# A gated linear attention, spectral mixer and conv gate on one core: the state update computed for each head's own 48 value columns only

## The chip, the cores and the metric

The kernel runs on one core of one Trainium2 chip. A core has a matrix engine (TensorE, in the profile PE, with its weight loads listed apart as PEld), a vector engine (VectorE, DVE), an activation engine (ScalarE, ACT), a general engine (GpSimd, POOL) and a synchronisation engine (SP) that issues the transfers here. They run side by side, each through its own list of instructions in order, and wait for each other by semaphores. SBUF is the working memory of 128 partitions; PSUM is the small memory that the matrix engine writes to. The metric is the device time of one execution in microseconds (us).

## The reference

Three stages follow one another on float32 data: a gated linear attention over 4 batches, 8 heads, 768 time steps and head dimension 48; a spectral mixer over time and channels; and a feed-forward part with a convolution of three taps and a gate. The change is in the first one.

```python
def _attn_ref(q, k, v, alpha):
    B, H, S, D = q.shape                       # 4, 8, 768, 48
    state = np.zeros((B, H, D, D))
    for t in range(S):
        state = alpha[:, :, t, :, None] * state + np.einsum('bhd,bhe->bhde', k[:, :, t], v[:, :, t])
        y[:, :, t] = np.einsum('bhd,bhde->bhe', q[:, :, t], state)

def _moe_ref(x, w_theta, w_tok_r, w_tok_i, w_ch):
    theta = x @ w_theta
    y = einsum('ts,bsd->btd', w_tok_r, x * cos(theta)) + einsum('ts,bsd->btd', w_tok_i, x * sin(theta))
    u = x + y
    return u + maximum(u @ w_ch, 0)

def _moe2_ref(x, w_in, conv_w, w_out):
    h = maximum(x @ w_in, 0)
    return (h * sigmoid(conv3(h, conv_w))) @ w_out
```

Each head has a state of 48 by 48 numbers. A head's state never meets another head's values.

## The kernel before

The 768 time steps of a batch are cut into 6 chunks of 128 (`NC`), so there are 24 chunks, numbered `ci`. Below, chunk n is the chunk with `ci` = n; chunks 0 to 5 are batch 0, 6 to 11 batch 1. Heads go in pairs: a tile holds the 48 channels of one head in partitions 0 to 47 and those of its partner in partitions 64 to 111 (a "column tile of 64" for the matrix engine), for 4 pairs (`NP`).

For each chunk, `a_prep` runs two scans on the vector engine (L229, L234), each of 4 segments of 129 columns, and multiplies q and k by their results (L243). `a_score` transposes k (`kps`, L252), makes the scores (`sc`), copies them (`pt`, L261) and masks them on GpSimd (L262). `a_y` makes the output of the chunk in PSUM: 32 matrix instructions from the masked scores (`y<-v_t,pt`, 48 columns) and, from the second chunk of a batch on, 16 from the state (`y<-S,qk_t`, 96 columns). `a_xt` transposes it (`xps`) and copies it to `u` (L321). `a_theta` makes the sines and cosines: `zh` (a rounded copy by ScalarE and the remainder by the vector engine, L71 to L73), the product `th`, then L343 to L348, then again a rounded copy `zh` and a remainder `zl`. `m_mix` is the mixing over time (`yps`); `u<-yps` (L374) empties its PSUM tiles.

The state update stands in the second half of `a_y`. A product of k (transposed, `kt`) and the values goes to the PSUM tile `kv`, in 8 matrix calls, each of which becomes 2 instructions, so 16 for a chunk. The values of both heads of the pair, 96 columns, are multiplied with either head's k, so half of what arises is never used. `tst` = old state + `kv` over partitions 0 to 111 and all 384 columns is one vector instruction (L296). Then GpSimd multiplies, once for each half of the partitions, the head's own 48 columns of each pair by the decay of the next chunk (`ftot`) into the new state `S` (L304). In the first chunk of a batch there is no old state: ScalarE copies the two used halves of `kv` into `S` (L301), and GpSimd multiplies in place.

The order on each engine is not the order of the source. The program is laid out by a scheduler that simulates times of its own, so a change in a few instructions moves others. All small PSUM tiles (`kps`, `sc`, `y`, `kv`, `xps`, `th`) share five buffers of one pool (`ps_a`) in turn: a new one waits until the reader of the fifth last one is done. The mixing has three buffers of its own (`ps_m`). The scan L229 writes a tile with one buffer (`fbt`), which the ScalarE instruction L240 reads, so the scan of a chunk waits for the L240 of the chunk before it.

From about 262 us on, the attention is over, and the rest (mixing of the last batch, `cps`, `hps`, `ops`) is the feed-forward part.

Of the kernel before, what the change touches and what calls it, by code (L numbers as in the profile page):

```python
# [8 lines left out]
F32 = mybir.dt.float32  # L9
# [6 lines left out]
ALU = mybir.AluOpType  # L16
PSUM = bass.MemoryType.PSUM

P = 128
B, H, S, D = 4, 8, 768, 48  # L20
DM = H * D
DFF = 1024
NP = H // 2
# [21 lines left out]
def tile_gated_linear_attention__then__spectral_moe__then__conv_gate(  # L45
# [14 lines left out]
    nc = tc.nc  # L60
    NCH = B * NC

    def mm(o, lhsT, rhs, start, stop):
        nc.tensor.matmul(o, lhsT, rhs, start=start, stop=stop, skip_group_check=True)  # L64
# [34 lines left out]
    def body(top, slow):  # L99
# [46 lines left out]
        with ExitStack() as ph1:  # L146
# [27 lines left out]
            def apool(name, bufs, **kw):  # L174
                return att_ctx.enter_context(tc.tile_pool(name=name, bufs=bufs, **kw))
# [4 lines left out]
            att = None if slow else apool("att", 2, side="right")  # L180
            x_p = apool("x", XB, side="right")
            zf_p = apool("zf", ZF, side="right")
            ps_a = apool("ps_a", 5, space=PSUM)
# [85 lines left out]
            def a_y(ci):  # L269
                qh, kh, ftot, vt = prep.pop(ci)  # L270
                pts, kt = scored.pop(ci)
                c = ci % NC
                Sp, Sn = Sst[ci % 2], Sst[(ci + 1) % 2]
                y = ps_a.tile([P, DM], F32, tag="a", name="y")
                halves = [slice(64 * i, 64 * i + 64) for i in range(2)]
                for p in range(NP):
                    for j in range(2):
                        h = 2 * p + j
                        for t in halves:
                            mm(y[t, h * D : (h + 1) * D], pts[j][:, p, t], vt[:, h * D : (h + 1) * D], h == 0, c == 0)  # L280
                if c > 0:
                    for p in range(NP):
                        for t in halves:
                            mm(y[t, p * 96 : p * 96 + 96], qh[:, p, t], Sp[:, p, :], False, True)
                x = x_p.tile([P, DM], F32, tag="x", name="x")
                marks["x"] = nc.scalar.copy(x, y)
                xs[ci] = x
                if c < NC - 1:
                    kv = ps_a.tile([P, NP, 2 * D], F32, tag="a", name="kv")
                    for p in range(NP):  # L290
                        for t in halves:
                            mm(kv[t, p, :], kt[:, p, t], vt[:, p * 96 : p * 96 + 96], p == 0, True)
                    nft = prep[ci + 1][2]
                    if c > 0:
                        tt = att.tile([P, NP, 2 * D], F32, tag="tst", name="tst", bufs=1)
                        nc.vector.tensor_tensor(tt[:112], Sp[:112], kv[:112], ALU.add)  # L296
                    else:
                        tt = Sn
                        for j in range(2):
                            r = slice(64 * j, 64 * j + D)  # L300
                            nc.scalar.copy(Sn[r, :, j * D : (j + 1) * D], kv[r, :, j * D : (j + 1) * D])  # L301
                    for j in range(2):
                        r = slice(64 * j, 64 * j + D)
                        nc.gpsimd.tensor_tensor(  # L304
                            Sn[r, :, j * D : (j + 1) * D],
                            tt[r, :, j * D : (j + 1) * D],
                            nft[r].unsqueeze(2).to_broadcast([D, NP, D]),
                            ALU.mult,
                        )
# [66 lines left out]
            def a_att(b, c):  # L376
                ci = b * NC + c
                if slow:
                    xs[ci] = x_p.tile([P, DM], F32, tag="x", name="x")
                    nc.sync.dma_start(out=xs[ci], in_=x_dram[b, c * P : (c + 1) * P, :])  # L380
                    a_xt(ci)
                    return
                if ci + 2 < NCH:
                    a_load(ci + 2)
                if ci + 1 < NCH:
                    a_prep(ci + 1)
                    a_score(ci + 1)
                a_y(ci)
                a_xt(ci)
# [306 lines left out]
```

## Time and profile before

| | us |
|---|---|
| median of 3 runs | 580.08 (578.15 to 581.35) |
| the profiled execution | 579.94 |
| its span, first to last instruction | 578.2 |
| PE busy | 553.1 (96%) |
| PEld busy | 532.9 (92%) |
| DVE busy | 457.1 (79%) |
| ACT busy | 338.4 (59%) |
| POOL busy | 93.6 (16%) |

The mean granted clock of TensorE is 0.978 of full speed. A line of a timeline gives the start, the length, the engine, the source line, the operation, what it writes and reads, its size and how many in a row were merged (x16); in square brackets stands how long the engine was idle before it and what ended that. The length of merged matrix instructions reaches to the modelled end of the last one, which overlaps the next instruction's start; so the pace is read from start to start. Times of GpSimd are rough.

### The profile page before, as it was taken

How to read it: one execution, taken by the hardware profiler on the slowest of the kernel's cores; microseconds unless marked ns; L12 is line 12 of the kernel's file. 1: busy time of each engine (PE TensorE's matmuls, PEld its weight loads, DVE VectorE, ACT ScalarE, POOL GpSimd, SP SyncE). 2: the span in 40 equal slices, each digit the busy share in tenths (PEclk: the TensorE clock that was granted, in tenths of full speed). 3: DMA queues.
4: the chain of work that ended last, by engine and by line, in shares of the span. 5: the costliest groups of instructions: out<-in, count | busy, mean ns of one | idle time of the engine just before them, and what ended most of it. 6: DMA issues, size and time to landing. Idle time of an engine off the chain costs nothing.

```text
span 578.2 us, 10973 instructions
## 1 busy us (share of the span) xinstructions
PE 553.1 (96%) x4407; PEld 532.9 (92%) x4407; DVE 457.1 (79%) x688; ACT 338.4 (59%) x695; POOL 93.6 (16%) x99
## 2 busy tenths in 40 slices
PE   6878989989999999999999999999999999999995
PEld 3767879979999999999999999999999999999995
DVE  7899997899856676542658889997888889798780
ACT  3665655555864567542752345567776776667561
POOL 2447514341044400350000000000000000000000
PEclk9688998999999999999999999999999999999999
DMA  8454652564024500320014333401044544546001
GB/s 322 153 170 136 212 187 81 174 220 161 1 83 139 174 20 8 97 64 1 1 31 160 111 112 109 145 20 41 5 147 139 176 137 144 198 143 204 27 29 46
DMA packets 24986, 65.41 MB, mean 113 GB/s; under 512 B 2528, under 2 KB 8672, under 8 KB 24544
## 3 DMA queue, kind: packets, MB, share of 16 engines
q1 hardware_dynamic: 24928, 64.64, 33.9%
q8 instruction: 36, 0.59, 0.4%
q14 instruction: 22, 0.18, 0.1%
HBM read 59.92 MB, written 4.72 MB: 112 GB/s over the span
## 4 chain that ended last, share of the span: by engine, by line
PE 80%; DVE 3%; issue 1%; ACT 1%; ACTq 0%
PE yps L64 23%; PE hps L64 18%; PE ops L64 18%; PE cps L64 7%; PE th L64 5%; PE y L64 4%; PE sc L64 3%; PE kv L64 2%; PE xps L320 1%; PE kps L252 1%; DVE fbt L229 1%; DVE stage L116 1%; DVE fbt L234 0%; DVE wtok L73 0%; DVE stage L115 0%
## 5 line engine op out<-in xcount | busy, mean ns | idle before, releaser
L64 PE MATMUL yps<-wtok,zh 128*128 128x384 f32 x576 | 153.0, 343 | 0.0
L64 PEld LDWEIGHTS yps<-wtok,zh 128*128 128x128 f32 x576 | 105.2, 191 | 2.4 <-ACT pt L261 0.2
L64 PE MATMUL hps<-x,win 128*128 128x386 f32 x576 | 107.1, 339 | 0.0
L64 PE MATMUL ops<-wout,g 128*128 128x384 f32 x576 | 106.9, 338 | 0.0
L64 PEld LDWEIGHTS hps<-x,win 128*128 128x128 f32 x576 | 102.2, 189 | 0.0
L64 PEld LDWEIGHTS ops<-wout,g 128*128 128x128 f32 x576 | 101.7, 187 | 0.0
L64 PE MATMUL yps<-wtok,zl 128*128 128x384 f32 x288 | 96.9, 339 | 0.0
L262 POOL TENSOR_SCALAR_AFFINE_SELECT pt<-pt 128x512 f32<-128x512 f32 x48 | 53.8, 1142 | 147.6 <-ACT pt L261 147.6
L64 PEld LDWEIGHTS yps<-wtok,zl 128*128 128x128 f32 x288 | 54.4, 189 | 0.8
L521 ACT ACTIVATE cv<-cv 128x384 f32<-128x384 f32 x64 | 33.4, 523 | 32.1 <-DVE cv L518 32.1
L229 DVE TENSOR_TENSOR_SCAN fbt<-a_t,onehot 128x516 f32<-128x516 f32 x24 | 29.5, 1229 | 22.9 <-ACT a_t L240 21.2
L73 DVE TENSOR_TENSOR g<-cv,g 128x384 fp32r<-128x384 f32 x64 | 35.5, 555 | 14.8 <-ACT g L72 14.2
L64 PE MATMUL th<-wth,zh 128*128 128x384 f32 x216 | 44.0, 340 | 0.0
L515 DVE SCALAR_TENSOR_TENSOR cv<-hh,cw,cv 128x383 f32<-128x383 f32 (+1 forms) x64 | 38.3, 613 | 4.4 <-ACT cv L512 4.1
L522 DVE SCALAR_TENSOR_TENSOR cv<-cv,hh 128x384 f32<-128x384 f32 x64 | 35.2, 556 | 7.9 <-ACT cv L521 5.9
L512 ACT ACTIVATE cv<-hh,cw 128x384 f32<-128x384 f32 x64 | 38.3, 616 | 3.8 <-DVE g L73 3.3
L64 PE MATMUL cps<-us,wch 128*128 128x384 f32 x216 | 40.3, 339 | 0.0
L72 ACT CAST g<-cv 128x384 fp32r<-128x384 f32 x64 | 32.6, 509 | 11.6 <-DVE cv L522 10.1
L518 DVE SCALAR_TENSOR_TENSOR cv<-hh,cw,cv 128x384 f32<-128x384 f32 (+1 forms) x64 | 38.4, 614 | 0.7
L64 PEld LDWEIGHTS cps<-us,wch 128*128 128x128 f32 x216 | 38.0, 188 | 0.5 <-issue 0.3
L64 PEld LDWEIGHTS th<-wth,zh 128*128 128x128 f32 x216 | 37.4, 188 | 0.5 <-DVE zh L73 0.4
L64 PE MATMUL sc<-qk_t 48*128 48x128 f32 x384 | 34.3, 294 | 3.1 <-DVE tst L296 2.5
(84 smaller groups left out, 826.8 us busy)
## 6 DMA issues: line engine op xcount, KB each, us to landing
qk_t<-in_qka_dram SPq DMA_DIRECT2D x24, 512.0 KB, 4.6
stage<-in_w_tok_dram SPq DMA_DIRECT2D x12, 768.0 KB, 4.5
top<-in_w_tok_dram SPq DMA_DIRECT2D x12, 768.0 KB, 4.3
a_t<-in_qka_dram SPq DMA_DIRECT2D x24, 260.0 KB, 2.8
v_t<-in_v_dram SPq DMA_DIRECT2D x24, 192.0 KB, 3.9
out_dram<-ob SPq DMA_DIRECT2D x24, 192.0 KB, 1.9
stage<-in_w_in_dram SPq DMA_DIRECT2D x4, 768.0 KB, 5.8
stage<-in_w_out_dram SPq DMA_DIRECT2D x4, 768.0 KB, 4.4
```

The source lines that it names most:

```text
L64: nc.tensor.matmul(o, lhsT, rhs, start=start, stop=stop, skip_group_check=True)
L72: cast = nc.scalar.copy(hi, src)
L73: lo_eng.tensor_tensor(lo, src, hi.bitcast(F32), ALU.subtract)
L116: nc.vector.scalar_tensor_tensor(fb, hi, 0xC0000000, fb, ALU.bitwise_and, ALU.bitwise_or)
L229: nc.vector.tensor_tensor_scan(bf[:, AW:0:-1], at[:, AW:0:-1], of[:, AW:0:-1], 0.0, ALU.mult, ALU.add)
L252: nc.tensor.transpose(kps[:, p, :], kh[:, p, :], ident)
L262: nc.gpsimd.affine_select(pt, pt, [[0, NP], [1, P]], ALU.is_ge, 0.0, base=0, channel_multiplier=-1)
L512: nc.scalar.activation(cv, hh[:, o : o + HALF], AF.Copy, scale=cw[:, f, 1:2])
L515: nc.vector.scalar_tensor_tensor(cv[:, a:HALF], hh[:, o + a - 1 : o + HALF - 1], cw[:, f, 0:1], cv[:, a:HALF], ALU.mult, ALU.add)
L518: nc.vector.scalar_tensor_tensor(cv[:, 0:e], hh[:, o + 1 : o + 1 + e], cw[:, f, 2:3], cv[:, 0:e], ALU.mult, ALU.add)
L521: nc.scalar.activation(cv, cv, AF.Tanh, scale=0.5)
L522: nc.vector.scalar_tensor_tensor(cv, cv, 1.0, hh[:, o : o + HALF], ALU.add, ALU.mult)
```

## The change

The tile `kv` is 48 columns wide for each pair instead of 96. Each of the 8 matrix calls takes only the values of the head whose k it uses, so 16 instructions of 48 columns stand where 16 of 96 stood. `tst` is compact too: 48 columns for each pair. It is made by two vector instructions, one for each half of the partitions (48 partitions, 192 columns each), where one of 112 partitions and 384 columns stood. GpSimd's two instructions read the compact tile. In the first chunk of a batch one ScalarE copy of 112 partitions and 192 columns fills `tst`, where two copies of 48 partitions and 192 columns into `S` stood, and GpSimd then writes `S` from `tst`.

```diff
-                    kv = ps_a.tile([P, NP, 2 * D], F32, tag="a", name="kv")
+                    kv = ps_a.tile([P, NP, D], F32, tag="a", name="kv")
                     for p in range(NP):
-                        for t in halves:
-                            mm(kv[t, p, :], kt[:, p, t], vt[:, p * 96 : p * 96 + 96], p == 0, True)
+                        for j, t in enumerate(halves):
+                            h = 2 * p + j
+                            mm(kv[t, p, :], kt[:, p, t], vt[:, h * D : (h + 1) * D], p == 0, True)
                     nft = prep[ci + 1][2]
-                    if c > 0:
-                        tt = att.tile([P, NP, 2 * D], F32, tag="tst", name="tst", bufs=1)
-                        nc.vector.tensor_tensor(tt[:112], Sp[:112], kv[:112], ALU.add)
-                    else:
-                        tt = Sn
-                        for j in range(2):
-                            r = slice(64 * j, 64 * j + D)
-                            nc.scalar.copy(Sn[r, :, j * D : (j + 1) * D], kv[r, :, j * D : (j + 1) * D])
+                    tt = att.tile([P, NP, D], F32, tag="tst", name="tst", bufs=1)
+                    if c == 0:
+                        nc.scalar.copy(tt[:112], kv[:112])
                     for j in range(2):
                         r = slice(64 * j, 64 * j + D)
+                        if c > 0:
+                            nc.vector.tensor_tensor(tt[r], Sp[r, :, j * D : (j + 1) * D], kv[r], ALU.add)
                         nc.gpsimd.tensor_tensor(
                             Sn[r, :, j * D : (j + 1) * D],
-                            tt[r, :, j * D : (j + 1) * D],
+                            tt[r],
                             nft[r].unsqueeze(2).to_broadcast([D, NP, D]),
                             ALU.mult,
                         )
```

The scheduler lays out the changed program anew. Three places matter here; source lines behind the change stand two lower than before. The first is the matrix engine around the state update of chunk 2, where `wtok_84` and `wtok_85` are the two parts of the mixing weights. Before:

```order
L64 MATMUL y<-S_111,qk_t 64x96 x8
L64 MATMUL kv<-v_t,kt 64x96 x8
L320 MATMUL xps<-ident,x 128x128 x3
L64 MATMUL th<-wth_115,zh 128x384
L64 MATMUL th<-wth_116,zh 128x384
```

and now:

```order
L64 MATMUL y<-S_111,qk_t 64x96 x8
L64 MATMUL kv<-v_t,kt 64x48 x8
L64 MATMUL yps<-wtok_84,zh 128x384
L64 MATMUL yps<-wtok_85,zh 128x384
L64 MATMUL yps<-wtok_84,zh 128x384
L64 MATMUL yps<-wtok_85,zh 128x384
L64 MATMUL yps<-wtok_84,zh 128x384
L64 MATMUL yps<-wtok_85,zh 128x384
L318 MATMUL xps<-ident,x 128x128 x3
```

Six mixing instructions of chunk 0 now stand ahead of the transpose of chunk 2. The second place is ScalarE in the same stretch, from the last step of the cosines of chunk 0 on (`zh<-zf` is the rounded copy that those six read). Before:

```order
L347 ACTIVATE zf<-zf,halfpi 128x384
L261 COPY pt<-sc 128x512 x2
L286 COPY x<-y 128x384
L266 COPY kt<-kps 128x512
L72 CAST zh<-zf 128x768
L321 COPY u<-xps 128x3x128
L72 CAST wtok_84<-stage 128x2x384
L240 ACTIVATE a_t,bacc<-fbt 128x1030
```

and now:

```order
L345 ACTIVATE zf<-zf,halfpi 128x384
L261 COPY pt<-sc 128x512
L72 CAST zh<-zf 128x768
L261 COPY pt<-sc 128x512
L286 COPY x<-y 128x384
L266 COPY kt<-kps 128x512
L319 COPY u<-xps 128x3x128
L72 CAST wtok_84<-stage 128x2x384
L240 ACTIVATE a_t,bacc<-fbt 128x1030
```

The rounded copy has moved ahead of the second score copy; `u<-xps` and L240 follow it as before. The third place is the vector engine at the end of batch 1's attention (144 to 151 us before). Before:

```order
L243 TENSOR_TENSOR qk_t<-qk_t,fbt 128x1024
L73 TENSOR_TENSOR zh<-u,zh 128x384
L348 TENSOR_TENSOR zf<-x,zf 128x768 x2
L73 TENSOR_TENSOR zh<-u,zh 128x384
L374 TENSOR_TENSOR u<-yps,u 128x384
L73 TENSOR_TENSOR zl<-zf,zh 128x768
L374 TENSOR_TENSOR u<-yps,u 128x384
```

and now:

```order
L243 TENSOR_TENSOR qk_t<-qk_t,fbt 128x1024
L346 TENSOR_TENSOR zf<-x,zf 128x768 x2
L73 TENSOR_TENSOR zl<-zf,zh 128x768
L73 TENSOR_TENSOR zh<-u,zh 128x384
L372 TENSOR_TENSOR u<-yps,u 128x384
L73 TENSOR_TENSOR zl<-zf,zh 128x768
```

The first remainder `zh` (chunk 9) has gone from here to a place some 6 us earlier, and the second one (chunk 10) now stands behind a `zl`. In the same stretch the matrix engine's list has the products `th` of chunks 6 to 9 in one run of 36, then 36 `yps`, then the `th` of chunk 10.

## Rows read from the trace of the kernel before

**Rows 1.** Stages: us, PE, PEld, DVE, ACT, POOL busy (x instructions), PEclk, DMA, GB/s.

```profile
27.40:97.20 69.80, 59.95 (x606) 54.64 (x607) 68.87 (x82) 43.46 (x88) 32.23 (x21) 0.90 0.51 162
97.20:133.30 36.10, 34.22 (x447) 31.42 (x443) 31.39 (x38) 19.27 (x42) 14.56 (x17) 1.00 0.59 186
133.30:262.00 128.70, 128.70 (x1373) 123.15 (x1373) 88.87 (x111) 78.39 (x161) 36.95 (x44) 1.00 0.25 81
262.00:578.20 316.20, 310.14 (x1803) 308.79 (x1801) 245.19 (x431) 183.10 (x377) 0.12 (x1) 1.00 0.29 97
```

**Rows 2.** Waits of the matrix engine: us in total, times, longest.

```profile
PE y L64 <- POOL S L304: 3.7, 2, 2.6
```

**Rows 3.** Timeline of the vector engine, chunks 2 and 3.

```profile
41.12 0.54 DVE L296 TENSOR_TENSOR tst<-S,kv 112x384 f32<-112x384 f32 x1
41.58 0.94 DVE L116 SCALAR_TENSOR_TENSOR stage<-stage 128x768 uint32<-128x768 uint32 x1
...
45.05 1.22 DVE L229 TENSOR_TENSOR_SCAN fbt<-a_t,onehot 128x516 f32<-128x516 f32 x1
46.20 0.79 DVE L73 TENSOR_TENSOR zh<-u,zh 128x384 fp32r<-128x384 f32 x1
...
47.38 0.17 DVE L233 RECIPROCAL starts<-fbt 128x4 f32<-128x4 f32 x1
47.58 1.23 DVE L234 TENSOR_TENSOR_SCAN fbt<-a_t,starts 128x516 f32<-128x516 f32 x1
...
53.25 0.56 DVE L296 TENSOR_TENSOR tst<-S,kv 112x384 f32<-112x384 f32 x1 [0.29 <-PE kv L64]
```

**Rows 4.** Groups by line and shape: busy us, mean ns, idle before.

```profile
L117 DVE SCALAR_TENSOR_TENSOR stage<-stage 128x768 uint32<-128x768 uint32 x22 | 21.2, 962 | 0.3
...
L296 DVE TENSOR_TENSOR tst<-S,kv 112x384 f32<-112x384 f32 x16 | 8.7, 544 | 6.2 <-PE kv L64 6.2
...
L117 DVE SCALAR_TENSOR_TENSOR stage<-stage 128x384 uint32<-128x384 uint32 x2 | 1.1, 558 | 0.0
```

**Rows 5.** Timeline of GpSimd: the state's two instructions in chunks 2 and 13.

```profile
41.74 5.62 POOL L304 TENSOR_TENSOR S<-tst,ftot 48x192 f32<-48x192 f32 x2 [0.95 <-DVE tst L296]
...
170.04 1.08 POOL L304 TENSOR_TENSOR S<-tst,ftot 48x192 f32<-48x192 f32 x2
```

**Rows 6.** Timeline around chunk 2: matrix engine and ScalarE.

```profile
39.59 0.55 PE L320 MATMUL xps<-ident,x 128*128 128x128 f32 x3 [1.09 <-ACT x L286]
...
40.32 0.84 ACT L72 CAST zh<-zf 128x768 fp32r<-128x768 f32 x1 [0.29 <-DVE zf L348]
41.06 0.47 ACT L321 COPY u<-xps 128x384 f32<-128x384 f32 x1
...
42.16 1.07 ACT L240 ACTIVATE a_t<-fbt 128x1030 bf16<-128x1030 f32 x1
```

**Rows 7.** Timeline of the matrix engine, chunks 6 and 7.

```profile
86.21 1.55 PE L64 MATMUL kv<-v_t,kt 128*64 128x96 f32 x16 [2.63 <-DVE zf L344]
87.69 2.29 PE L64 MATMUL yps<-wtok,zh 128*128 128x384 f32 x6
89.77 0.84 PE L320 MATMUL xps<-ident,x 128*128 128x128 f32 x3
...
95.85 1.14 PE L64 MATMUL y<-v_t,pt 128*64 128x48 f32 x32
96.82 0.85 PE L64 MATMUL y<-S,qk_t 128*64 128x96 f32 x16
97.50 0.83 PE L64 MATMUL kv<-v_t,kt 128*64 128x96 f32 x16
```

**Rows 8.** Timeline at 144 to 148 us: vector engine and matrix engine.

```profile
144.64 1.87 DVE L348 TENSOR_TENSOR zf<-x,zf 128x768 f32<-128x768 f32 x2
146.43 0.55 DVE L73 TENSOR_TENSOR zh<-u,zh 128x384 fp32r<-128x384 f32 x1
...
147.37 0.94 DVE L73 TENSOR_TENSOR zl<-zf,zh 128x768 fp32r<-128x768 f32 x1
...
147.04 1.48 PE L64 MATMUL th<-wth,zh 128*128 128x384 f32 x7
```

## The prediction

> **What bounds the kernel now.** I read the table by stages first. Its third and fourth rows show a matrix engine that is busy throughout from 133 to 262 us, and all but 6 us of the rest [rows 1]: there the time is the sum of its instructions, and the vector engine, at 89 of 129 us, has room. Its first row shows the opposite for 27 to 97 us: the vector engine is busy 68.87 of 69.80 us, while the matrix engine lacks 9.9 us and is granted 0.90 of its full clock. Between, from 97 to 133 us, the vector engine has 31.4 of 36.1 us, and the matrix engine lacks 1.9. The matrix engine's last large gap, 2.63 us before chunk 6's `kv`, is ended by a vector instruction [rows 7]. So a delay of the vector engine before 86 us reaches the end undiminished, unless matrix work shrinks; one at 105 to 130 us reaches it nearly; one after 151 us costs nothing; and a shorter matrix instruction pays only where that engine is the late one, from 86 to 103 us and from 133 us on.
>
> **The matrix instructions.** In chunk 7, start to start, 32 instructions of 48 columns take 0.97 us (30 ns each) and 16 of 96 columns 0.68 us (42.5 ns) [rows 7]. Sixteen at 30 ns take 0.48, so a chunk saves 0.20 us. The ten state updates after 133 us save 2.0 us. [...] The bounds are no saving at all (if loading the weights sets the pace) and half the time, 0.34 us for a chunk.
>
> **Two vector instructions for one.** The trace has no vector instruction of 192 columns. From 768 to 384 columns one kind falls from 962 to 558 ns, 1.05 ns a column [rows 4]; 192 fewer than 544 ns gives 0.34 us. Neighbours without a wait overlap by 0.08 us: L296 starts at 41.12 and the next at 41.58, 0.46 later [rows 3]. If the two halves overlap like that, they take 2 x 0.26 = 0.53, 0.07 more than now. If each starts only when the one before is done, at a distance of 0.03 as L234 behind L233 (47.55 to 47.58), they take 2 x 0.37 = 0.74, 0.28 more. I take 0.28: the halves start in different partitions, and every vector row of before starts at partition 0, so the overlap seen there need not hold.
>
> [...]
>
> **GpSimd between them.** In chunk 2 GpSimd's two state instructions take 5.62 us, against 1.08 in chunk 13 [rows 5]. [...] Chunks 1 to 4 give 4 x 0.43 = 1.7 us. [...]
>
> [...]
>
> In chunks 8 to 10 (105 to 130 us) GpSimd already delays the vector engine after `tst`, so only the 0.28 is new: 3 x 0.28 = 0.85 us. After 151 us nothing counts.
>
> **Chunk 2's new order.** The six `yps` need the rounded copy `zh`, which ends at 41.16 now [rows 6] and about 0.3 later then (chunk 1's delay). The matrix engine, done with `kv` at about 38.2, stands for over 3 us, where now it goes on with `xps` at 39.59. After 2.63 us of standing it ran at half pace: six `yps` in 2.08 us [rows 7]. So 41.5 + 2.1, then `xps` with 0.64: `u<-xps` starts at 44.3 instead of 41.06. L240 starts 1.10 behind it [rows 6] or a little more, at 45.5, and ends at 46.6; the scan L229 waits for it. The vector engine would be there at 45.05 + 0.33 + 0.43 = 45.8. It stands for 0.8 to 0.9 us. If the matrix engine were back at full pace at once, this would be near 0; I take 0.9. By the time of chunk 3's `kv` (about 51.2 by the same steps) the matrix engine has caught up, so the vector engine's wait of 0.29 at 53.25 [rows 3] goes: -0.3.
>
> **Chunk 10's remainder.** At 147.04 the matrix engine's `th` starts 0.06 us after `zh` ends at 146.98 [rows 8]: no slack. In the new order (one `zh` gone, one `zl` put in front) this `zh` ends at about 147.8, before other delays. The matrix engine has by then two instructions fewer behind it, 0.17 us each. 0.8 + 0.35 = 1.15 us are lost for good; the bound on the other side is 0.
>
> **Chunk 0.** One ScalarE copy less (0.33 us) is mostly lost, since the next instruction there waits for the vector engine: -0.1. The later three first chunks have ScalarE to spare.
>
> The sum: 1.7 + 0.9 - 0.3 - 0.1 = +2.2 at 86 us; -0.6 to 103 us; +0.85 to 130 us; +1.15 at 147 us; -2.0 to the end: **+1.6 us**. The profiled execution took 579.94 (span 578.2 and 1.7 around it), so 581.5; it lies 0.14 below the median, so **581.7**, 0.3% slower. The measurement can tell about 0.5% (2.9 us) from no change: under 577.2 is faster, over 583.0 slower.
>
> **Rivals.**
> 1. *The matrix saving decides (faster).* The halves overlap (4 x 0.07), GpSimd doesn't get between, chunk 2's gap is covered and chunk 10's `zh` is too: 0.3 - 0.3 - 0.1 - 0.6 + 0.2 - 2.0 = -2.5, so 577.6. For it speaks that the matrix engine bounds 445 us of the span; against it, that four covers must all hold. Chance 0.19.
> 2. *Chunk 2's gap leaves the matrix engine slow until `kv` of chunk 3 (slower).* If it stays at half pace, then from 44.2: nine `th` 3.1, `kps` 0.85, four `yps` 1.4, 16 `sc` 2.9, 32 `y` 1.75, 16 `y<-S` 1.3 and `kv` 0.9 end at 56.4. The vector engine needs `kv` at 53.3, and waits 3.1 us: 584.8. It decides from where the engine reaches `kv` after 53.3. For it: chunk 6's half pace lasted from 86.2 past `xps` at 89.77 [rows 7]. Against it: the chunk's later instructions are dense. Chance 0.16.
> 3. *The change doesn't shorten `kv`:* the 64-column weight loads set the pace, 42 ns stay, the 2.6 us of savings go: 584.3. Against it, the 30 ns of `y` with the same weight loads. Chance 0.05.
>
> **How the numbers follow.** My forecast has 0.60, with its own range 579.2 to 584.2 (the bounds of the four delays, mostly one or two of them off). Rival 1 reaches below 577.2 in over half of its cases and the forecast hardly does: faster 0.14. Slower takes rivals 2 and 3 (0.19) and a quarter of the forecast's 0.60: 0.34. The rest, 0.52, is no change. The range of 8 in 10 reaches from near the centre of rival 1 to just beyond rival 2: 577.4 to 585.4.
>
> **What would show it.** Right: `kv` of 16 in about 0.5 us start to start from 160 us on; `tst` twice, at a distance of about 0.37, and the following vector instruction longer by about 0.2 in chunks 1 to 4; the first GpSimd half short (0.5 us) there and the second long; a matrix gap of about 3 us before the first `yps` and an idle vector engine before chunk 3's L229; the `th` of chunk 10 waiting for DVE `zh`; the last gap before chunk 6's `kv` ending near 88.4. Wrong: that gap ending at 86 or earlier, a `kv` that stays at 0.68 us, or new gaps of the matrix engine after 160 us, which I hold to be nil.

## The result and the profile after

The changed kernel takes 582.97 us (median of 9 runs, 582.30 to 584.55), the kernel before 579.63 beside it (9 runs, 578.13 to 581.62). The ratio is 1.0054, 95% interval 1.0037 to 1.0072: 3.1 us slower (2.1 to 4.2). The forecast was 581.7 with 1.6 us of loss, its range 577.4 to 585.4. The profiled execution took 582.52, span 580.7. In the runs further down, one execution of 883.58 us and one of the kernel before of 680.48 us, at granted clocks of 0.556 and 0.745, are left out of medians and ratios.

The stages of the kernel after, with the columns of [rows 1]:

```profile
27.40:97.20 69.80, 57.31 (x592) 52.77 (x593) 68.94 (x85) 42.02 (x84) 19.52 (x21) 0.88 0.51 164
97.20:133.30 36.10, 32.70 (x445) 29.40 (x442) 32.18 (x42) 17.99 (x38) 12.61 (x16) 1.00 0.55 178
133.30:262.00 128.70, 126.95 (x1370) 121.41 (x1370) 91.08 (x118) 79.30 (x162) 35.21 (x41) 1.00 0.27 84
262.00:580.70 318.70, 311.74 (x1821) 310.44 (x1817) 246.53 (x434) 183.37 (x379) 2.20 (x5) 1.00 0.29 96
```

The first stage is still the vector engine's (68.94 of 69.80 us). GpSimd fell from 32.23 to 19.52. New is the third row: where the matrix engine had no gap, it now lacks 1.75 us of its 128.70.

Matrix engine, chunks 6 and 7, answering [rows 7]; idle time and what ended it in brackets. First the row behind chunk 7's `kv` in the kernel before, then the kernel after:

```profile
98.25 0.45 PE L64 MATMUL yps<-wtok,zh 128*128 128x384 f32 x1
```

```profile
87.69 1.05 PE L64 MATMUL kv<-v_t,kt 128*64 128x48 f32 x16 [2.02 <-DVE zf L342]
...
97.78 0.62 PE L64 MATMUL kv<-v_t,kt 128*64 128x48 f32 x16
98.33 0.44 PE L64 MATMUL yps<-wtok,zl 128*128 128x384 f32 x1
```

The 16 instructions take 0.55 us start to start (97.78 to 98.33), where they took 0.75 (97.50 to 98.25): the 0.20 of the forecast. Chunk 6's `kv` starts 1.48 later than before.

Vector engine, chunks 1 to 3, answering [rows 3]:

```profile
33.02 0.73 DVE L301 TENSOR_TENSOR tst<-S,kv 48x192 f32<-48x192 f32 x2
33.78 0.98 DVE L73 TENSOR_TENSOR wtok<-stage,wtok 128x768 fp32r<-128x768 f32 x1
34.68 1.53 DVE L229 TENSOR_TENSOR_SCAN fbt<-a_t,onehot 128x516 f32<-128x516 f32 x1
36.14 0.53 DVE L73 TENSOR_TENSOR zh<-u,zh 128x384 fp32r<-128x384 f32 x1
...
44.05 1.11 DVE L117 SCALAR_TENSOR_TENSOR stage<-stage 128x768 uint32<-128x768 uint32 x1
45.08 1.26 DVE L73 TENSOR_TENSOR wtok<-stage,wtok 128x768 fp32r<-128x768 f32 x1
46.27 1.22 DVE L229 TENSOR_TENSOR_SCAN fbt<-a_t,onehot 128x516 f32<-128x516 f32 x1
```

The pair takes 0.73 us and the next instruction starts 0.76 after the pair's start, where one instruction gave 0.46: 0.30 more. The state's GpSimd instructions, answering [rows 5]:

```profile
33.44 1.68 POOL L302 TENSOR_TENSOR S<-tst,ftot 48x192 f32<-48x192 f32 x2 [5.20 <-DVE tst L301]
...
43.84 1.68 POOL L302 TENSOR_TENSOR S<-tst,ftot 48x192 f32<-48x192 f32 x2
```

Both halves are through in 1.68 us, where chunk 2 took 5.62. In chunk 1 the first starts 0.42 after the pair's start, and the vector instruction beside it is hardly longer (0.98, where the kernel before has 0.95); the second holds the scan up by 0.30 (1.53 against 1.23), and `zh` no longer pays (0.53 where [rows 3] has 0.79). In chunk 2 the first starts at 43.84, 0.55 after the pair's start, and the instruction beside it takes 1.11 us, where such an instruction takes some 0.95 without a neighbour [rows 3]; the one beside the second takes 1.26. The matrix engine's wait for S [rows 2] is gone from the waits.

Around chunk 2, answering [rows 6], with ScalarE's rows below the matrix engine's:

```profile
41.96 1.31 PE L64 MATMUL yps<-wtok,zh 128*128 128x384 f32 x6 [2.02 <-ACT zh L72]
43.11 0.55 PE L318 MATMUL xps<-ident,x 128*128 128x128 f32 x3
...
43.70 0.48 ACT L319 COPY u<-xps 128x384 f32<-128x384 f32 x1 [0.44 <-PE xps L318]
...
44.81 1.06 ACT L240 ACTIVATE a_t<-fbt 128x1030 bf16<-128x1030 f32 x1
```

L240 ends at 45.87, the scan follows at 46.27, and the vector engine does not stand. Answering [rows 8], at 148 to 151 us:

```profile
149.73 0.61 PE L64 MATMUL th<-wth,zh 128*128 128x384 f32 x2 [1.29 <-ACT zh L72]
150.78 1.50 PE L64 MATMUL th<-wth,zh 128*128 128x384 f32 x7 [0.43 <-DVE zh L73]
...
149.17 0.51 ACT L72 CAST zh<-u 128x384 fp32r<-128x384 f32 x1
...
150.18 0.55 DVE L73 TENSOR_TENSOR zh<-u,zh 128x384 fp32r<-128x384 f32 x1
```

Here the matrix engine stands for 1.29 us, until ScalarE's copy `zh<-u` of 149.17 is done, and for 0.43 us, until the vector engine's remainder is. And a gap that no term of the forecast has, in the feed-forward part:

```profile
360.38 4.92 PE L64 MATMUL cps<-us,wch 128*128 128x384 f32 x27
366.33 2.00 PE L64 MATMUL cps<-us,wch 128*128 128x384 f32 x10 [1.03 <-ACT us L72]
```

### The profile page after: what moved, and what is told of

Read it like the earlier page. It is cut to its first block, busy times and chain, and to the rows that moved or that the text cites. A ratio compares the mean times of both kernels' runs of the same rounds, so it can differ in the third digit from the quotient of the medians.

```text
span 580.7 us, 11015 instructions
## 1 busy us (share of the span) xinstructions
PE 548.2 (94%) x4407; PEld 529.0 (91%) x4407; DVE 460.7 (79%) x704; ACT 337.0 (58%) x691; POOL 79.1 (14%) x99
## 4 chain that ended last, share of the span: by engine, by line
PE 75%; DVE 6%; issue 2%; DMA 1%; ACT 1%
PE yps L64 21%; PE hps L64 18%; PE ops L64 18%; PE cps L64 7%; PE th L64 4%; PE y L64 4%; PE sc L64 2%; PE kv L64 1%; DMA stage<-in_w_tok_dram 1%; DVE fbt L234 1%; PE xps L318 1%; DVE stage L116 1%; DVE fbt L229 1%; PE kps L252 1%; DVE wtok L73 1%
## 5 line engine op out<-in xcount | busy, mean ns | idle before, releaser
L64 PE MATMUL yps<-wtok,zh 128*128 128x384 f32 x576 | 150.8, 341 | 3.2 <-ACT zh L72 2.0
L262 POOL TENSOR_SCALAR_AFFINE_SELECT pt<-pt 128x512 f32<-128x512 f32 x48 | 52.5, 1114 | 169.4 <-ACT pt L261 169.3
L64 PE MATMUL th<-wth,zh 128*128 128x384 f32 x216 | 47.0, 356 | 1.7 <-ACT zh L72 1.3
L64 PEld LDWEIGHTS th<-wth,zh 128*128 128x128 f32 x216 | 39.7, 199 | 2.8 <-ACT zh L72 1.6
```

The source lines that it names most:

```text
L262: nc.gpsimd.affine_select(pt, pt, [[0, NP], [1, P]], ALU.is_ge, 0.0, base=0, channel_multiplier=-1)
```

## The experiments

The program builder puts the instructions into another order as soon as `kv` is 48 columns wide, whether the sum is one vector instruction or two. So the change has three parts: the width of `kv`, the pair, and the order. The runs take them one by one. The runs with `in_order` in their diffs hold every engine to a listed order by dependences without a wait; their line numbers stand 107 to 109 higher, those of the others a few at most. The pair alone and the narrow product with one sum in the new order have no list: the builder gives them these orders by itself, the new one exactly on the matrix and vector engines, the old one but for a single instruction each on the matrix engine, ScalarE and the vector engine. "Both, in the old order" has this same order. In all of them but the change itself and the run on chunk 2, the first chunk of a batch keeps the two ScalarE copies of the kernel before.

| run | `kv` columns | sums | order | ratio to before, 95% | us |
|---|---|---|---|---|---|
| pair alone | 96 | 2 | old | 1.0024, 1.0005 to 1.0043 | +1.4 |
| narrow alone | 48 | 1 | old | 0.9959, 0.9931 to 0.9987 | -2.4 |
| narrow alone, again | 48 | 1 | old | 0.9949, 0.9920 to 0.9978 | -3.0 |
| both | 48 | 2 | old | 1.0001, 0.9979 to 1.0023 | +0.1 |
| the change, again | 48 | 2 | new | 1.0072, 1.0033 to 1.0110 | +4.2 |
| narrow, one sum | 48 | 1 | new | 1.0027, 1.0001 to 1.0053 | +1.6 |
| new order alone | 96 | 1 | new | 1.0064, 1.0038 to 1.0089 | +3.7 |

The last column is the ratio less 1, times 580. Each ratio is to the kernel before on the same chip; the runs stand on three chips, so ratios are compared, not times. The kernel before held to its own list was not run; that a list by itself costs nothing is shown only so far that the stretch from chunk 12's `kv` to the first `cps` takes 159.0 us in the changed kernel and also in the one run of it with a list.

### The pair alone

```diff
-                        nc.vector.tensor_tensor(tt[:112], Sp[:112], kv[:112], ALU.add)
+                        for j in range(2):
+                            r = slice(64 * j, 64 * j + D)
+                            js = slice(j * D, (j + 1) * D)
+                            nc.vector.tensor_tensor(tt[r, :, js], Sp[r, :, js], kv[r, :, js], ALU.add)
```

> Two theories of the 3.2 us that the change costs. Pair theory: the second vector instruction of each state update costs 0.30 us in every chunk that the vector engine bounds, and that is the loss. Order theory: once the kv instructions are 48 columns wide the program builder puts the instructions into another order, and that order is the loss. Here the kv product stays 96 columns wide and the order stays that of the kernel before; only the sum is computed in two instructions (48 partitions by 192 columns each). Pair theory: 1.2 us late at 86 us, 1.2 to 3 us at the end, so 581.2 to 583. Order theory: within 0.5 us of the kernel before.

Measured: 581.47 us, +1.4 us (0.3 to 2.5). The pair costs something by itself, but not 3.1. Since the instructions around the state update stand in the order of before, this run also shows what a chunk pays. Vector engine, chunk 2, beside [rows 3]:

```profile
42.76 0.72 DVE L299 TENSOR_TENSOR tst<-S,kv 48x192 f32<-48x192 f32 x2
43.51 0.98 DVE L116 SCALAR_TENSOR_TENSOR stage<-stage 128x768 uint32<-128x768 uint32 x1
44.42 1.26 DVE L73 TENSOR_TENSOR zl<-zf,zh 128x768 fp32r<-128x768 f32 x1
...
48.48 0.53 DVE L73 TENSOR_TENSOR zh<-u,zh 128x384 fp32r<-128x384 f32 x1
...
49.72 1.47 DVE L234 TENSOR_TENSOR_SCAN fbt<-a_t,starts 128x516 f32<-128x516 f32 x1
```

From `tst` to the second scan it is 6.96 us (42.76 to 49.72), where [rows 3] has 6.46 (41.12 to 47.58): 0.50 more, and 0.49 to 0.52 in chunks 1, 3 and 4. The pair makes 0.29 of it and the instruction beside GpSimd's first half 0.03; the one beside the second half loses 0.31 (1.26 against 0.95), and some 0.15 come back behind `zh`. In chunks 8 to 10 the run falls behind by 0.31, 0.14 and 0.03. That is 2.5 us on the vector engine, less the wait of 0.29 ahead of chunk 3's `tst` [rows 3], which is gone here; the interval of the time just holds it.

### The narrow product alone

The changed kernel's `kv` with one sum, and the order of the kernel before. `ORDER` holds, for each engine, the positions of that kernel's instructions.

```diff
+                        nc.vector.tensor_tensor(
+                            tt[:112].rearrange("q p (j e) -> q p j e", j=2),
+                            Sp[:112].rearrange("q p (j e) -> q p j e", j=2),
+                            kv[:112].unsqueeze(2).to_broadcast([112, NP, 2, D]),
+                            ALU.add,
+                        )
...
+        for a, b in zip(seq, seq[1:]):
+            tc.add_manual_dep(
+                log[b],
+                log[a].name,
+                mybir.DependencyInfo(mybir.DependencyClass.NoSync, mybir.DependencyReason.DATA),
+                reason="issue order",
+            )
...
     run(False)
+    in_order(tc)
```

> The kv product is computed 48 columns wide, but one vector instruction (112 partitions by 384 columns, which reads the compact product twice) still forms the sum, and every engine is held to the order of the kernel before by dependences without a wait. That leaves the saving of the matrix instructions alone: 16 of 12 ns in each of 20 chunks. My forecast of that term: 2.0 us after 133 us and 0.3 to 0.6 us ahead of it, so 577.4 to 578.0 us by either theory. If the matrix engine only waits as much longer: 579.5 to 580.5 us.

Measured: 577.66 us, -2.4 us (0.8 to 4.0). It is the matrix saving. The stretch from chunk 12's `kv` to the first `cps` shows it without the vector engine. The timeline's row of that `kv` and the view of the tile `cps` (with the start of its first and last instruction), of the kernel before and then of this run:

```profile
158.45 0.85 PE L64 MATMUL kv<-v_t,kt 128*64 128x96 f32 x16
```

```profile
L64 PE MATMUL cps<-us,wch x216: 336/337/419, 318.5 to 506.4; 128*128 128x384 f32 x108
```

```profile
156.38 0.64 PE L171 MATMUL kv<-v_t,kt 128*64 128x48 f32 x16
```

```profile
L171 PE MATMUL cps<-us,wch x216: 336/337/418, 314.3 to 502.0; 128*128 128x384 f32 x108
```

160.05 us (318.5 - 158.45) became 157.92, 2.1 less; 10 x 0.20 = 2.0 was the forecast's term. Other executions repeat it within 0.02: the stretch takes 160.1 us in the pair alone, and 157.9 in this kernel's second run and with both in the old order.

### Both, in the old order

```diff
+                        if c > 0:
+                            nc.vector.tensor_tensor(tt[r], Sp[r, :, j * D : (j + 1) * D], kv[r], ALU.add)
...
     run(False)
+    in_order(tc)
```

> The changed state update whole (48 columns wide, two vector instructions), with every engine held to the order of the kernel before. Pair theory: nearly what the changed kernel takes, 1 to 3 us over the kernel before less the 2.0 us of the matrix instructions, 580 to 582. Order theory: the 2.0 us of the matrix instructions are all that is seen, 577.5 to 578.5 us.

Measured: 580.10 us, +0.1 us (-1.2 to 1.3): as the pair theory had forecast the time. In the old order the change as written is neutral within 1.3 us, which leaves some 3 us of its loss to the order. In this run the `th` that waits in [rows 8]'s place stands for 0.17 us:

```profile
147.58 1.66 PE L172 MATMUL th<-wth,zh 128*128 128x384 f32 x8 [0.17 <-DVE zh L181]
```

### The change, again

No edit.

> The changed kernel as it is, beside the three others on the same chip. Both theories: 3.1 us over the kernel before, 582.9 us.

Measured: 583.49 us, +4.2 us (1.9 to 6.4), on the chip of the three runs above. Its interval lies above that of the run before.

### Narrow, one sum, new order

The diff of the narrow product alone, without `in_order`.

> The kv product 48 columns wide and one vector instruction, as in the run that had the narrow product alone, but in the order into which the program builder puts it by itself, which on the matrix engine is that of the changed kernel. From the runs so far: the pair costs 1 to 2.5 us, the matrix instructions give back 2.4 us, and the order costs 3.3 us. Order theory: 0 to 1.5 us over the kernel before, 580 to 581.5. If the order costs only where the pair already makes the vector engine late: 577.5 to 578.5.

Measured: 581.81 us (median of 11), ratio +1.6 us (0.1 to 3.1). Narrow alone gives -2.4, the new order brings it to +1.6: 4.0 us, with no pair in either.

### The new order alone

```diff
     run(False)
+    in_order(tc)
```

This is the kernel before with the other list of positions.

> The kernel before, each of its instructions unchanged, but held to the order that the narrower kv instructions bring about. Order theory: 2.5 to 3.5 us over the kernel before (582.5 to 583.8), with the matrix engine idle for 1.3 and 0.4 us at 150 us and for 1.0 us at 366 us as in the changed kernel. Pair theory: no change, within 1 us.

Measured: 585.05 us, ratio +3.7 us (2.2 to 5.2). The order theory holds, and the loss is rather above its 2.5 to 3.5. The waits of the matrix engine (total, times, longest) have the changed kernel's stands at the same places, though not one instruction differs from the kernel before; the one ahead of `cps` is ended here by the vector engine:

```profile
PE yps L172 <- ACT zh L180: 1.9, 1, 1.9
PE cps L172 <- DVE u L574: 1.3, 1, 1.3
...
PE th L172 <- ACT zh L180: 0.8, 1, 0.8
PE th L172 <- DVE zh L181: 0.4, 1, 0.4
```

And here the vector engine does stand in chunk 2. First the matrix engine's row, then ScalarE's `L240` (here L348), then the vector engine's:

```profile
42.84 2.29 PE L172 MATMUL yps<-wtok,zh 128*128 128x384 f32 x6 [1.86 <-ACT zh L180]
...
46.92 1.06 ACT L348 ACTIVATE a_t<-fbt 128x1030 bf16<-128x1030 f32 x1
...
47.05 0.96 DVE L181 TENSOR_TENSOR wtok<-stage,wtok 128x768 fp32r<-128x768 f32 x1 [1.46 <-ACT wtok L180]
48.10 1.23 DVE L337 TENSOR_TENSOR_SCAN fbt<-a_t,onehot 128x516 f32<-128x516 f32 x1
```

The six `yps` take 2.29 us at a granted clock of 0.50, the pace of [rows 7], where the changed kernel's took 1.31 at 1.00. `xps` and `u` follow later, ScalarE's `wtok` stands behind `u`, and the vector engine waits 1.46 us for it. L240 stands behind `wtok` and ends at 47.98; the scan, which needs it, starts at 48.10, so it could hardly have started earlier without the wait for `wtok` either. The narrow product with one sum in the new order shows the same (2.29 and 1.47 us); in the change run again the six took 1.59, and the vector engine stood for 0.31.

### The feed-forward part in the old order

The changed kernel with a list whose positions are its own up to the first cast `us`, and the old ones behind it.

> The changed kernel, with the order of the kernel before from the first cast of the feed-forward part (us) on, and its own order ahead of that. If the idle stretch of the matrix engine at 366 us (1.0 to 1.5 us, before cps, which waits for the cast of us) comes from the order there: it is gone and the time is 1.0 to 1.5 us under that of the changed kernel, 581.5 to 582.5. If a late start of that part makes it: no change, 583.

Measured: 582.33 us, +2.0 us over before (0.8 to 3.1), 1.2 to 2.2 under the changed kernel's two measurements. The idle stretch is gone:

```profile
361.08 4.92 PE L173 MATMUL cps<-us,wch 128*128 128x384 f32 x27
365.84 1.75 PE L173 MATMUL hps<-x,win 128*128 128x386 f32 x9
367.43 1.75 PE L173 MATMUL cps<-us,wch 128*128 128x384 f32 x9
```

The old order has nine `hps` between the two groups of `cps`; the new one goes from `cps` to `cps`, and the second group's `us` is not cast yet. So the gap is the order's. The interval overlaps that of the changed kernel, so the size rests on the trace. In this execution, too, the vector engine stood in chunk 2, behind six `yps` of 2.29 us:

```profile
46.08 0.96 DVE L182 TENSOR_TENSOR wtok<-stage,wtok 128x768 fp32r<-128x768 f32 x1 [1.01 <-ACT wtok L181]
```

### Chunk 2 in the old order

```diff
+                        if b == 0 and h == 0 and c == 0 and not slow:
+                            behind(first, (("yS", 3),))
```

`first` is the first `yps` instruction, `("yS", 3)` the last `y<-S` of chunk 3.

> The changed kernel with one dependence without a wait more: the first yps products of chunk 0 are issued behind the y products of chunk 3, so that the 2 us in which the matrix engine waits for zh at 42 us go. My forecast's term for chunk 2's new order (0.9 us, less 0.3): 0.6 us faster than the changed kernel, 582.3. By the trace of the changed kernel, where the vector engine was not idle behind that stretch: no change, within 0.3 us of 582.9.

Measured: 582.99 us, +2.3 us over before (0.9 to 3.7), 0.9 to 1.9 under the changed kernel. The intervals overlap: the time agrees with the forecast's term, but does not show it. Nor does the edit bring the whole of the old order back: it moves `yps` on the matrix engine, while ScalarE's list stays the new one but for one `kt`, and the matrix engine now stands in the same place for `x`, ahead of `xps`:

```profile
42.12 0.90 PE L321 MATMUL xps<-ident,x 128*128 128x128 f32 x3 [4.17 <-ACT x L289]
```

The rows of the new order alone show the term better.

### The pair by columns, and in four

```diff
+                            ps = slice(2 * j, 2 * j + 2)
+                            nc.vector.tensor_tensor(tt[:112, ps], Sp[:112, ps], kv[:112, ps], ALU.add)
```

> The kernel before with its one sum cut in two by columns (112 partitions by 192 columns each, both from partition 0) instead of by partitions (48 by 192, from partitions 0 and 64). If the 0.30 us that the pair costs comes of two instructions that write one tile one behind the other, whatever their partitions: the pair again takes 0.73 us, and the instruction behind it starts 0.76 us after the first. If the start at partition 64 or the engine's switch between partitions makes it: about 0.6 us.

```diff
+                            for ps in (slice(0, 2), slice(2, 4)):
+                                nc.vector.tensor_tensor(tt[r, ps, js], Sp[r, ps, js], kv[r, ps, js], ALU.add)
```

> Each half of 48 partitions cut once more by columns (48 by 96): two instructions from partition 0, then two from partition 64. If the change of the starting partition holds the next instruction: the second starts about 0.16 us after the first and the third about 0.25 after the second, then 0.16 and 0.25 again, and the next other instruction starts some 0.83 us after the first of the four. If 48 partitions in place of 112 keep instructions from overlapping: 0.25 each, 1.0 us in all.

Both were run for their trace alone. Vector engine, chunk 1; first the pair by columns, then the four. The last two rows are one group of four in a later chunk, seen through two windows that meet at 250 us, so that its second instruction stands in both:

```profile
34.06 0.61 DVE L298 TENSOR_TENSOR tst<-S,kv 112x192 f32<-112x192 f32 x2
34.59 0.95 DVE L73 TENSOR_TENSOR wtok<-stage,wtok 128x768 fp32r<-128x768 f32 x1
```

```profile
33.92 0.87 DVE L300 TENSOR_TENSOR tst<-S,kv 48x96 f32<-48x96 f32 x4
34.81 0.96 DVE L73 TENSOR_TENSOR wtok<-stage,wtok 128x768 fp32r<-128x768 f32 x1
...
249.72 0.41 DVE L300 TENSOR_TENSOR tst<-S,kv 48x96 f32<-48x96 f32 x2
249.90 0.70 DVE L300 TENSOR_TENSOR tst<-S,kv 48x96 f32<-48x96 f32 x3
```

By columns the next instruction starts 0.53 after the first half (34.06 to 34.59), 0.07 more than for one instruction: the smaller of the forecast's two figures. By partitions it starts 0.76 after (33.02 to 33.78 in the changed kernel). In the four, the second starts 0.18 after the first, from the same partition (249.72 to 249.90), while one of them takes 0.25; from the first to the instruction behind the four it is 0.89 (33.92 to 34.81), which leaves about 0.27 each time that the starting partition changes (0.18 + 0.27 + 0.18 + 0.27 = 0.90). So in these rows neither the count nor the 48 partitions go with the longer step, but the start in another partition does: about 0.27 against 0.18. The 0.76 by partitions and the 0.53 by columns agree with it.

### The narrow product alone, again

> The version that the runs so far point to, once more for a narrower interval: the kv product 48 columns wide, one vector instruction, every engine in the order of the kernel before. 2.0 to 2.6 us under the kernel before, ratio 0.9955 to 0.9965; at the least under 1.000.

Measured: 578.16 us, 0.9949: 3.0 us faster (1.3 to 4.6). With the first time, this is the version that beats the kernel before, and so the changed one.

## Why the prediction came out as it did

The time was inside the range and the sign was right. But the measured loss of 3.1 us (2.1 to 4.2) is nearly twice the forecast's 1.6, which lies outside that interval: the sum is some 1.5 us small, and not all of its parts held. That it came this near is partly luck, since it holds terms that are too large beside those that are too small or missing.

- *The matrix instructions* (-2.0 after 133 us): right in mechanism and size, 0.20 us a chunk and 2.1 us between chunk 12 and the first `cps`. No run shows the 0.6 us before 103 us as a gain: in the changed kernel `kv` takes, start to start, 0.20 less in chunk 7 (0.55 against 0.75) and 0.50 less in chunk 6 (0.98 against 1.48), but the stretch between the two differs by over 4 us between executions (below).
- *Two vector instructions for one* (0.28): 0.30 measured, and for the reason given, the start in another partition: by columns it is 0.07.
- *GpSimd between them* (0.43 a chunk, the pair inside it): this was the author's estimate, and no run shows it. In the same order 0.50 were measured, so it is right in size by luck and wrong in who pays. The first half does start early, yet the instruction beside it lost 0.03 us, not the 0.15 by which the 0.43 exceeds the pair (0.16 in chunk 2 of the changed kernel, where the half starts later). The second half is long, as forecast (1.11 us in chunks 1 and 2 of the changed kernel, the first 0.50); the instruction after the one beside the first half takes 0.30 more, which the sum has nowhere, and some 0.15 come back behind `zh`.
- *Chunks 8 to 10* (0.28 each, +0.85): too large. In the pair alone they cost 0.31, 0.14 and 0.03, about 0.5 in all.
- *Chunk 2's new order* (+0.9): right in mechanism, its size hangs on the clock. With the six `yps` in 2.29 us the vector engine stood for 1.46 (new order alone) and 1.01 us (feed-forward part in the old order), and the scan started behind L240 as forecast; in the changed kernel they took 1.59 and it stood for 0.31 in one execution, and 1.31 without a stand in the other. The forecast named both cases and took the slower one.
- *Chunk 10's remainder* (+1.15): right in place, too small, and only in part for the reason given. The matrix engine stands for 1.29 + 0.43 = 1.72 us there, for 0.8 + 0.4 in the new order alone and for 0.17 in the old order with the same pair. The vector engine's remainder ends only the smaller stand; the larger one is ended by ScalarE's copy `zh<-u`, which starts at 149.17 behind a `zh<-zf` (148.44) in the new order, and at 145.43 stood ahead of both of them before. The forecast did not look at ScalarE's list here.
- *After 160 us, "which I hold to be nil"*: wrong. The gap of 1.03 us at 366 us is the order's, shown by its going with the old order. The forecast read the new order at three places and did not look at the feed-forward part, where the change touches no line; its 1.03 us are about two thirds of the 1.5 that the sum is short.
- Rival 1's price (577.6) is what the narrow product alone took (577.66 and 578.16). Its condition was that the pair, the gap in chunk 2 and chunk 10 cost nothing; with one sum and the old order that kernel has none of the three, so it bears out the saving, not the rival.

By the runs, the parts are +1.4 (pair), -2.4 to -3.0 (matrix) and +3.7 (order): +2.1 to +2.7, within the uncertainty of the 3.1 measured. The order is the largest, and the forecast gave it 0.9 - 0.3 + 1.15 = 1.75. Left open: of the order's 3.7 us, the rows name 1.2 us at 150 us, 1.3 at 366 and 1.46 in chunk 2; how these add up in the median isn't shown, since chunk 2's share lies between 0 and 1.47 in the executions profiled.

## What to carry to other kernels

Where a program builder sets the order, a smaller instruction is also a new input to it: compare the order of every engine over the whole program, also where the change touches no line, and run the old order with the new instructions before judging the idea. Cut a vector instruction by columns rather than by partitions: here that was 0.07 against 0.30 us, and 0.06 against 0.50 with the delay by GpSimd's instructions behind it. And where an engine runs at either pace, as the matrix engine did here (six `yps` in 1.31 or 2.29 us), work out a delay for both and keep both in the range.

## What the runs showed of the hardware that was not expected

The stretch from chunk 6's `kv` to chunk 7's took 8.4 us in one execution of the narrow product alone (86.87 to 95.30) and 12.8 in another of the same kernel (86.00 to 98.75). A stretch with the columns of [rows 1] and the row of chunk 6's `kv`, first of the narrow product alone, then of its second run:

```profile
87.00:92.00 5.00, 5.00 (x45) 4.50 (x46) 4.97 (x6) 4.93 (x12) 4.15 (x4) 1.00 0.15 43
```

```profile
86.87 0.67 PE L171 MATMUL kv<-v_t,kt 128*64 128x48 f32 x16 [1.21 <-DVE zf L457]
```

```profile
87.00:92.00 5.00, 5.00 (x21) 4.55 (x20) 4.96 (x5) 4.67 (x11) 4.37 (x4) 0.50 0.17 43
```

```profile
86.00 1.09 PE L171 MATMUL kv<-v_t,kt 128*64 128x48 f32 x16 [2.62 <-DVE zf L457]
```

In the first the matrix engine had stood for 1.21 us and was granted its full clock behind it (1.00); in the second it had stood for 2.62 and was granted 0.50, and `kv` took 1.09 in place of 0.67 us. How long it stood does not decide this alone: ahead of the six `yps` of chunk 2 it stood for 2.02 us in the changed kernel, and they ran at a granted 1.00 (1.31 us); in the new order alone it stood there for 1.86, and they ran at 0.50 (2.29 us). What sets the granted clock is not shown here. Single executions therefore differ by more than this change costs, and differences of a few tenths were read here from stretches with one clock, or from medians.
